# Scaled R of group 0 read from SBUF, the float32 decay-column matmuls set beside the first layer, the last output row block in two column halves, and a new written-out order

## The chip, the cores and the metric

The kernel runs on one core of one Trainium2 chip. The metric is device microseconds of one execution. The core has five engines with instruction streams of their own: TensorE (PE, whose weight loads are listed apart as PEld), VectorE (DVE), ScalarE (ACT), GpSimd (POOL) and SyncE (SP), which here issues most of the DMA transfers. Tensors are worked on in SBUF; matmuls write to PSUM.

## The reference, cut to what matters

```python
# attention: batch 4, 8 heads, 768 steps, head size 48
for t in range(S):
    cur = einsum('bhd,bhe->bhde', u * k[t], v[t])
    y[t] = einsum('bhd,bhde->bhe', r[t], state + cur)
    state = w[:, :, None] * state + einsum('bhd,bhe->bhde', k[t], v[t])
# feed-forward on the 3072 rows of y (384 wide), 2048 hidden units
h = x @ w_in
g = where(h >= 1, h, where(h <= -1, 0, (h + 1)**2 / 4))
out = g @ w_out
```

The recurrence decays by `w` per step, for each head and channel. All inputs and the output are float32.

## The kernel before, in words

**Tiling.** The 768 steps are cut into 6 chunks of 128, and the 4 batches into 2 pairs. A *group* is one chunk of one batch pair: 12 groups, numbered 0 to 11, each with two *units* (one batch each), so that units 0 and 1 are group 0. Within a chunk the recurrence becomes matmuls: R is scaled by `w` to the power (t - 64) (table `Wup`), K by the power (63 - t) (table `Wdn`), and then the 128x128 product of scaled K and scaled R, masked to the lower triangle, times V gives the part inside the chunk; scaled R times the state gives the part from earlier chunks. The diagonal term with `u` is worked out apart and added.

**The steps of a group**, by the names of the order table: `LR`, `LK`, `LV` load R, K, V (line 252; half a group is 192 KB); `Rs`, `Ks` scale; `KU`, `RKU` multiply K by u and R by that; `us` sums it over each head (293); `V` casts V to bf16; `B` multiplies V by that sum (302); `TR`, `TK` or `T` transpose on PE (319), `cR`, `cK`, `c` copy the result to SBUF; from group 4 on `RT`, `KT` transpose by DMA instead (307); `A` is the product of K and R (359), `AT` masks it (373 for a half, 368 for a whole unit); `Sp` is K times V (394), `Tm`, `Tmg` and `decayg` update the state, `sbf`, `sbfg` cast it; `Y` is the result in PSUM (421, 427), `y`, `yg` add the diagonal term; `X` and `xc` transpose it on PE (449), or `xcg` by DMA (456), giving `xT`. The feed-forward part follows per group and quarter q of the hidden units: `m` is the first layer (464; 12 matmuls of 256 columns into `hp`), `r`, `s`, `g` the activation (475 on ACT or 472 on DVE, 484 on ACT, 487 on DVE), `M` the second layer for one unit and one quarter (499; 4 matmuls of 384 columns), `o`/`og` the copy out of PSUM, `st`/`stg` the store (515, 518).

**PSUM.** `m`, `M` and, later in the program, all others use four pairs of banks, given as the number behind the slash. `m0.3/0` uses pair 0 again after `m0.0/0`, so it waits until `g0.0` has read `hp`. In the first two groups most other tiles use four single banks b0 to b3; `m1.0/3` and `m1.2/2` take the same space later, so they wait for the last reader of these.

**The set-up.** `ln` takes the logarithm of w (one row). `bw` (206) and `bu` (210) spread that and u over 128 partitions by float32 matmuls with one row of ones. ACT makes the tables: `WdnS` (224) and `WupS` (221) into SBUF, `Wdn` (218) and `Wup` (214) a second time into PSUM, from where the scaling of group 0 reads them. `wq` (232) makes the decay column, w to the power 128 as a column, by four float32 matmuls of one column; `wE` and `wC` spread it to the mask `wCm`, which `Tm` needs. `Z` are matmuls of zeros (526); `WI` and `WO` load the weights of the two layers through POOL's own DMA queue, in three and two pieces (243, 246). Piece 0 of `WI` serves quarter 0, piece 1 quarter 1, piece 2 quarters 2 and 3.

**What sets the order.** The string ORDER is the program: each word is one step, each engine executes its words in the order in which they stand there, and waits come only from data and from buffers (SLOTS gives the buffers of each kind). `=V`, `=A`, `=G` choose DVE, ACT or POOL. Loads, DMA transposes and stores all stand in SP's queue, in order.

Of the kernel before, what the change touches and what calls it, by code (L numbers as in the profile page):

```python
# [25 lines left out]
TK0/0 Wup/1 Rs0.0=V TR0/3 LK1.1 cK0=A WupS KU0.1=G KU0.0=V RKU0.0=G cR0=A KU1.0=G LV0.1 Rs0.1=V Z2 TR1/1 A0/03 LV1.0
LV1.1 WI0 WI1 WI2 us0.0 cR1=A TK1/1 cK1=A AT0.1 Z4 A1/13 Rs1.0=V LR2.0 LR2.1 Rs1.1=V V0.1 AT1.0 V0.0 Z9 TR3/1 B0.0=G
AT1.1 RKU0.1=V wE AT0.0 wC=A us0.1 Z7 Y1/3 TR2/0 B0.1=G Y0/2 y0 y1 cR2=A RKU1.0=G Z8 X0/2 Z4 TK2/3 X1/0 Ks1.1=G xc0=A
Sp1/2 cK2=A xc1=A Z7 TK3/3 cK3=A Tm1 A2/20 m0.0/0 cR3=V us1.0 AT2.1 AT2.0 r0.0=A A3/31 AT3.1 KU1.1=G RKU1.1=G m0.1/1
V1.0 s0.0=A B1.0=G Sp2/2 AT3.0 us1.1 r0.1=A Tm2 Y2/3 y2 g0.0 V1.1 X2/0 LK2.0 Y3/1 B1.1=G s0.1=A LK2.1 Sp0/2 Sp3/3  # L30
xc2=V LK3 y3 WO0 m0.3/0 r0.3=A s0.3=A g0.1 X3/1 Tm0 xc3=V m0.2/1 LR3 LV2.0 Tm3 m1.1/2 g0.3 r1.1=V m1.0/3 m1.2/0 Ks2=G
r0.2=A s0.2=A g0.2 sbf2=A s1.1=A r1.0=A s1.0=A sbf3=A g1.1 m1.3/1 r1.2=V WO1 KU2=G LV2.1 M0.00/2 M0.10 M0.11 M0.01
g1.0 M1.00/3 M1.10 M1.11 M1.01 Rs2=G s1.2=A g1.2 T5/0 RKU2=G LK4 r1.3=A s1.3=A g1.3 T4/1 LV3 Ks3=G M0.02 M0.03 LR4 us2
c5=V A5/0 KU3=G Rs3=G c4=V A4/1 AT5 sbf1=A M1.02 M0.12 M0.13 AT4 T6/0 sbf0=A V2 Y4/1 Y5 B2=G og0=A T7/2 c6=A RKU3=G
c7=A yg2 LV5 M1.12 Sp4/0 Sp5 M1.03 X5/2 Tmg2 decayg2=G X4/1 M1.13 A6/0 xc4=A xc5=V m2.0/2 A7/1 us3 AT6 m2.1/0 og1=A
LK5 LR5 V3 Y6/3 B3=G sbfg2=A r2.0=A AT7 Y7 m2.2/1 s2.0=A Ks4=G yg3 xcg3 m2.3/3 g2.0 Rs4=G r2.1=A s2.1=A g2.1 LV4
r2.2=A s2.2=A KT4 M2.00/2 M2.10 M2.01 M2.11 r2.3=A KU4=G RT4 RKU4=G g2.2 s2.3=A LK6 m3.0/0 us4 M2.02 m3.1/1 LR6 M2.12
LV6 r3.0 s3.0=A Ks5=G g2.3 M2.03 Sp6/3 Sp7 M2.13 g3.0 m3.2/0 Rs5=G Tmg3 r3.1 s3.1=A RT5 og2=A g3.1 V4 AA4/23 AT9 Ks6=G
r3.2 s3.2=A KT5 m3.3/1 M3.00/3 M3.10 V5 B4=G AT8 Y8/2 Y9 r3.3 g3.2 s3.3=A LK8 M3.11 M3.12 M3.01 M3.02 yg4 AA5/20 g3.3
M3.13 M3.03 xcg4 m4.0/1 LR7 KU5=G RKU5=G AT10 LK7 decayg3=G sbfg3=A Rs6=G og3=A us5 LV7 B5=G KU6=G RKU6=G r4.0 Sp8/2  # L40
Sp9 AT11 Tmg4 m4.1/3 s4.0=A Y10/0 Y11 yg5 m4.2/2 r4.1 g4.0 xcg5 RT6 s4.1=A g4.1 m4.3/0 r4.2 us6 KT6 r4.3 LV8 s4.2=A
g4.2 M4.00/1 M4.10 M4.01 stg0 M4.11 s4.3=A g4.3 m5.1/3 Ks7=G V7 M4.12 LR8 decayg4=G Rs7=G AA6/02 M4.02 M4.03 M4.13
r5.1 AT12 m5.0/0 s5.1=A V6 sbfg4=A stg2 AT13 Y12/2 Y13 stg1 og4=V m5.2/1 g5.1 KU8=G B6=G yg6 m5.3/3 KT7 xcg6 Sp10/2
r5.0 s5.0=A KU7=G RKU7=G r5.2 s5.2=A Sp11 g5.0 M5.00/0 M5.10 M5.11 M5.01 RT7 Tmg5 LR9 g5.2 M5.02 Ks8=G LK9 us7 r5.3
s5.3=A V8 g5.3 decayg5=G sbfg5=A LK11 m6.1/2 r6.1 s6.1=A stg3 Rs8=G RT8 B7=G AA7/13 M5.03 Rs9=G M5.12 M5.13 AT15
m6.0/3 og5=A r6.0 AT14 g6.1 Y14/0 Y15 yg7 RKU8=G KU9=G xcg7 s6.0=A m6.3/1 m6.2/2 g6.0 Sp12/0 Sp13 r6.3 r6.2 s6.2=A us8
KT8 M6.00/3 M6.10 M6.11 M6.01 Tmg6 LV11 B8=G s6.3=A m7.1/0 RT9 LK10 g6.2 M6.02 LV10 g6.3 AA8/21 M6.03 r7.1 M6.12 M6.13
decayg6=G AT16 sbfg6=A RKU9=G LR10 s7.1=A AT17 Ks9=G og6=A m7.0/2 Sp14/1 Sp15 Y16/3 Y17 r7.0 g7.1 m7.2/0 KU11=G s7.0=A
Tmg7 yg8 xcg8 Ks10=G KT9 r7.2 m7.3/1 g7.0 M7.00/3 s7.2=A g7.2 M7.10 M7.11 LV9 r7.3 M7.01 KU10=G s7.3=A g7.3 V10 stg6
decayg7=G M7.12 RKU10=G sbfg7=A M7.02 AA9/02 M7.13 m8.0/1 stg5 LR11 AT18 Rs10=G V9 KT10 M7.03 r8.0 s8.0=A AT19 RT10  # L50
og7=V us9 B9=G m8.1/0 m8.2/2 r8.1 s8.1=A Y18/3 Y19 stg7 g8.0 m8.3/1 yg9 r8.2 Rs11=G RKU11=G M8.00/3 M8.10 xcg9 g8.1
M8.11 s8.2=A g8.2 Sp16/0 Sp17 Tmg8 stg4 RT11 r8.3 s8.3=A M8.01 M8.02 g8.3 m9.0/2 r9.0 s9.0=A us10 decayg8=G AA10/01
AT21 Ks11=G M8.03 sbfg8=A B10=G AT20 M8.12 M8.13 g9.0 og8=A m9.1/1 Y20/0 Y21 r9.1 m9.2/3 s9.1=A yg10 xcg10 g9.1 r9.2
M9.00/0 m9.3/2 KT11 s9.2=A stg8 M9.10 M9.11 Sp18/1 Sp19 r9.3 g9.2 s9.3=A M9.01 Tmg9 M9.02 g9.3 m10.0/3 decayg9=G V11
# [512 lines left out]
```

## Time and profile before

| what | value |
|---|---|
| median of 3 runs | 174.38 us (174.08, 174.38, 174.93) |
| the profiled execution | 173.8 us, its span 172.0 us |
| DVE, ACT, POOL busy | 76%, 76%, 68% of the span |
| DMA, mean over the span | 164 GB/s |
| first layer, 576 matmuls | 69.1 us |
| second layer, 384 matmuls | 68.4 us |

The profiled execution took 1.8 us more than its span, which is the time outside the first and last instruction. Busy time on PE is an overlap of pipelined matmuls, so the start of one group of matmuls against the start of the next says more than its length. Rows of the timeline give the start, the length, the engine with the line, what is written and read, a count, and in brackets the idle time just ahead with what ended it.

### The profile page before, as it was taken

What the parts mean: (1) busy time and instruction counts of PE and PEld (TensorE: products, weight loads), DVE (VectorE), ACT (ScalarE), POOL (GpSimd) and SP (SyncE); (2) the same over time, 40 slices, a digit from 0 to 9 for tenths busy, and PEclk for the clock granted to TensorE, in tenths of its full rate; (3) what the DMA queues carried; (4) which work ended last, traced back from release to release, by engine and by line L of the source; (5) the groups of instructions that cost most, each with busy time, mean ns of one, the idle gap of its engine ahead of it and who ended that gap; (6) DMA issues with size and microseconds to landing.
All of it is one profiled execution on the core that took longest, in us unless ns stands there. A gap on an engine that the chain in (4) does not pass through costs nothing.

```text
span 172.0 us, 4014 instructions
## 1 busy us (share of the span) xinstructions
PE 163.7 (95%) x1658; PEld 130.9 (76%) x1658; DVE 130.6 (76%) x149; ACT 130.0 (76%) x150; POOL 117.1 (68%) x85
## 2 busy tenths in 40 slices
PE   7989968999999999989999999999999999999991
PEld 5768768956889778588787797696897787888850
DVE  4578798988687688859799779885889958873751
ACT  4356588991699899289979878689695896988941
POOL 3496755998589959999999998999577804300000
PEclk9999999999999999999999999999999999999999
DMA  5999999999995999999999998998999034130022
GB/s 106 198 187 191 199 203 197 221 195 203 174 190 88 213 188 175 188 204 150 200 312 197 185 215 174 219 173 168 308 195 219 4 60 138 43 98 0 8 91 91
DMA packets 103591, 28.26 MB, mean 164 GB/s; under 512 B 98834, under 2 KB 102676, under 8 KB 103572
## 3 DMA queue, kind: packets, MB, share of 16 engines
q1 hardware_dynamic: 101824, 24.85, 79.6%
q0 software_dynamic: 1744, 3.15, 10.0%
...
q10 hardware_dynamic: 4, 0.00, 0.0%
...
## 4 chain that ended last, share of the span: by engine, by line
PE 81%; DMA 5%; SPq 4%; ACT 3%; POOL 2%; DVE 2%; issue 1%; DVEq 0%; POOLq 0%
PE hp L464 36%; PE op L499 34%; SPq L252 4%; PE A L359 3%; DMA Vi<-in_v_dram 3%; DMA xT<-y 2%; PE Y L427 2%; PE Y L421 2%; PE Sp L394 2%; ACT pt L475 1%; ACT Vb L111 1%; POOL V L302 1%; PE T L319 1%; DVE g L487 1%; POOL RKU L271 1%
## 5 line engine op out<-in xcount | busy, mean ns | idle before, releaser
L464 PE MATMUL hp<-xT,w_in 128*128 128x256 bf16 x576 | 69.1, 273 | 0.9 <-DMA xT<-y 0.5
L499 PE MATMUL op<-w_out,g 128*128 128x384 bf16 x384 | 68.4, 326 | 0.0
L487 DVE SCALAR_TENSOR_TENSOR g<-sq,hp 128x1024 bf16<-128x1024 bf16 x48 | 57.9, 1215 | 13.2 <-ACT sq L484 13.2
L464 PEld LDWEIGHTS <-w_in 128*128 128x128 bf16 x576 | 61.9, 114 | 4.2 <-issue 1.2
L475 ACT ACTIVATE pt<-hp 128x1024 f32<-128x1024 f32 x46 | 46.9, 1020 | 14.0 <-PE hp L464 14.0
L499 PEld LDWEIGHTS <-g 128*128 128x128 bf16 x384 | 36.3, 98 | 21.3
L484 ACT ACTIVATE sq<-pt 128x1024 bf16<-128x1024 f32 x46 | 48.3, 1057 | 1.2
L368 DVE TENSOR_TENSOR AT<-A,umask 128x1024 bf16<-128x1024 f32 x20 | 23.7, 1219 | 5.2 <-PE A L359 5.2
L271 POOL TENSOR_TENSOR Ks<-Ki,Wdn 128x768 bf16<-128x768 f32 (+1 forms) x12 | 20.2, 1684 | 7.4 <-DMA Ki<-in_k_dram 3.7
L302 POOL TENSOR_TENSOR V<-Vb,diag 128x768 f32<-128x768 bf16 (+1 forms) x14 | 18.1, 1292 | 10.2 <-DVE diag L293 4.4
L271 POOL TENSOR_TENSOR RKU<-Ri,KU 128x768 f32<-128x768 f32 (+1 forms) x13 | 21.2, 1631 | 1.2 <-DVE KU L271 0.8
L405 POOL TENSOR_TENSOR state<-Tm,wCm 128x768 f32<-128x768 f32 x8 | 14.6, 1822 | 10.6 <-DVE Tm L402 10.6
L271 POOL TENSOR_TENSOR KU<-Ki,u_sb 128x768 f32<-128x768 f32 (+1 forms) x13 | 21.2, 1632 | 0.4 <-DMA Ki<-in_k_dram 0.3
L271 POOL TENSOR_TENSOR Rs<-Ri,Wup 128x768 bf16<-128x768 f32 x10 | 18.2, 1824 | 0.0
L439 DVE TENSOR_TENSOR y<-Y,V 128x768 bf16<-128x768 f32 x10 | 9.6, 956 | 5.9 <-PE Y L427 3.3
L111 ACT CAST Vb<-Vi 128x768 bf16<-128x768 f32 (+1 forms) x14 | 10.2, 734 | 4.8 <-DMA Vi<-in_v_dram 4.8
L293 DVE TENSOR_REDUCE diag<-RKU 128x16 f32<-128x768 f32 (+1 forms) x14 | 11.6, 830 | 1.5 <-POOL RKU L271 1.5
L111 ACT COPY o<-op 128x768 f32<-128x768 f32 (+1 forms) x9 | 6.9, 764 | 6.4 <-PE op L499 6.3
L111 ACT CAST state_bf<-state 128x768 bf16<-128x768 f32 (+1 forms) x12 | 8.5, 717 | 3.7 <-POOL state L405 3.7
L427 PE MATMUL Y<-Vb,AT 128*128 128x48 bf16 x192 | 10.2, 185 | 0.4 <-ACT Vb L111 0.4
L427 PEld LDWEIGHTS <-AT 128*128 128x128 bf16 x192 | 9.3, 97 | 0.7 <-issue 0.5
L402 DVE TENSOR_TENSOR Tm<-Sp,state 128x768 f32<-128x768 f32 x8 | 7.6, 956 | 2.7 <-PE Sp L394 2.7
...
## 6 DMA issues: line engine op xcount, KB each, us to landing
out_dram<-o SPq DMA_DIRECT2D x11, 384.0 KB, 3.9
Ki<-in_k_dram SPq DMA_DIRECT2D x9, 384.0 KB, 6.0
Ri<-in_r_dram SPq DMA_DIRECT2D x9, 384.0 KB, 6.1
Vi<-in_v_dram SPq DMA_DIRECT2D x9, 384.0 KB, 5.0
w_out<-in_moe_w_out_dram POOLq DMA_DIRECT2D x2, 768.0 KB, 8.6
Ki<-in_k_dram SPq DMA_DIRECT2D x6, 192.0 KB, 3.9
Ri<-in_r_dram SPq DMA_DIRECT2D x6, 192.0 KB, 4.6
Vi<-in_v_dram SPq DMA_DIRECT2D x6, 192.0 KB, 5.4
```

What stands on the lines that cost most here:

```text
L111: nc.scalar.copy(out, in_) if e == "A" else engines[e].tensor_copy(out, in_)
L271: engines[e].tensor_mul(part(out)[:, :, :, :D], part(a), rep(b, j1 - j0) if len(b.shape) == 3 and b.shape[1] == H else part(b))
L293: nc.vector.tensor_reduce(d[:, hs], tiles["RKU", g][:, hs, :], AX.X, ALU.add)
L302: engines[e].tensor_mul(t[:, hs, :], tiles["V", g][:, hs, :], tiles["diag", g][:, hs].unsqueeze(2).to_broadcast([P, n, D]))
L368: nc.vector.tensor_mul(t.rearrange("p i n t -> p (i n) t"), tiles["A", n].rearrange("p i (n t) -> p (i n) t", t=P), umask.unsqueeze(1).to_ ...
L405: engines[e].tensor_mul(states[g % BP], tiles["Tm", g], flat(wCm).unsqueeze(1).to_broadcast([P, UNITS, DM]))
L427: nc.tensor.matmul(Y[:, h * D : (h + 1) * D], AT[:, i, p, :], V[:, j * H + h, :], start=(c == 0), stop=True, skip_group_check=True,)
L464: nc.tensor.matmul(hp[:, f, :], w_in_sb[wi][:, i, wo * FG * P + f : (wo + 1) * FG * P : FG], tiles["xT", g][:, :, i, :], start=(i == 0), s ...
L475: nc.scalar.activation(t, tiles["hp", g, q], AF.Relu, bias=0.5, scale=0.5)
L484: nc.scalar.activation(t, p, AF.Square)
L487: nc.vector.scalar_tensor_tensor(out=make("g", ("g", g, q), [P, FG, TOK], BF16), in0=tiles["sq", g, q], scalar=1.0, in1=tiles["hp", g, q], ...
L499: nc.tensor.matmul(tiles[key][:, k, :DO], tiles["g", g, q][:, f, j * P : (j + 1) * P], w_out_sb[wi][:, wo, f * DO : (f + 1) * DO], start=( ...
```

## The change

1. `Wup` (the PSUM copy) goes out of the order; `WupS` stands ahead, and both units' scaled R of group 0 are read from the SBUF table, as those of all other groups are. `Wdn` in PSUM stays.
2. `wq` moves from behind `bu` to the place between the last transpose of group 0 (`X1`) and `m0.0`; `wE` and `wC` follow there.
3. In group 11 each unit's output is kept in two column halves in the two banks of its pair: 192-column matmuls, 8 in place of 4 for each quarter. The last step is cut into `MA`, `MB` with a copy and a store for each half (`oA`, `oB`, `stA`, `stB`).
4. The order is written anew throughout: other PSUM pairs, other places of loads and of zeros (60 of them before, 64 now), and some steps on another engine, among them `KU0.1`, `KU2`, `KU3` and `Ks3` from POOL to DVE, `uS` from DVE to ACT, `Rs1.1` from DVE to POOL. The number of loads, stores of whole groups, and all arithmetic stay.
5. The buffer `idle` shrinks from 512 to 128 columns. The new steps `HR`, `HK`, `Zq` are defined but not in the order.

```diff
-Zs/0 ln Z19 bw/1 LK0.0 bu/0 uS=V LK1.0 LR0.0 LK0.1 LR0.1 LV0.0 wq/2 WdnS Ks1.0=G LR1.0 LR1.1 Wdn/3 Ks0.0=V Ks0.1=V
+Zs/1 LV0.0 LR0.0 LR1.0 ln LK0.0 Z9 bw/0 LK0.1 bu/2 WupS LR0.1 Rs0.0=V Rs1.0=V Z2 TR0/1 uS=A Wdn/2 LV0.1 KU0.0=V
...
-M11.10/0
-M11.11 g11.2 stg10 r11.3 s11.3=A M11.00/3 M11.01 M11.12 M11.02 g11.3 M11.13 M11.03 o11.1=V st11.1 o11.0=A st11.0
+M11.00/0 M11.01 s11.3=A og10=V g11.3 M11.10/3 stg10 M11.11 M11.02 M11.03 M11.12 o11.0=V MA11.13 st11.0 MB11.13
+oA11.1=A oB11.1=V stA11.1 stB11.1
...
-    idle = const.tile([P, 512], BF16, name="idle")
+    idle = const.tile([P, P], BF16, name="idle")
...
-    def do_M(e, b, g, jq):
+    def do_M(e, b, g, jq, halves=(0, 1)):
...
-        key, k = (("op", g, j), 0) if last else (("op", g), j)
+        key = ("op", g, j) if last else ("op", g)
...
+        for i, o0, o1 in [(i, i * DO // 2, (i + 1) * DO // 2) for i in halves] if last else [(j, 0, DO)]:
+            for f in range(FG):
+                nc.tensor.matmul(
+                    tiles[key][:, i, : o1 - o0], tiles["g", g, q][:, f, j * P : (j + 1) * P], w_out_sb[wi][:, wo, f * DO + o0 : f * DO + o1],
+                    start=(q == 0 and f == 0), stop=(q == nQ - 1 and f == FG - 1),
+                )
...
+    def half_out(e, g, j, i):
+        cols = slice(i * DO // 2, (i + 1) * DO // 2)
+        copy(e, make("o", ("o", g, j), [P, UNITS, DO], F32)[:, 0, cols], tiles["op", g, j][:, i, : DO // 2])
...
+    def half_st(g, j, i):
+        cols = slice(i * DO // 2, (i + 1) * DO // 2)
+        nc.sync.dma_start(out=rows_out(g, j, j + 1)[:, :, cols], in_=tiles["o", g, j][:, 0:1, cols])
```

PE, the place of the decay column `wp`. Before, it stands in the set-up, between the two spreading matmuls and the first transposes (`TK`):

```order
L526 MATMUL z<-idle 128x128
L206 MATMUL lwp<-lnw,ones 128x384
L210 MATMUL up<-u_row,ones 128x384
L232 MATMUL wp<-ones,lnw 128x1 x4
L319 LDWEIGHTS Ks
L319 MATMUL TK<-ident,Ks 128x128
```

PE now, where the first layer (`hp`) begins; `X` are the transposes of group 0's result, one set for each unit:

```order
L566 MATMUL z<-idle 128x128
L460 LDWEIGHTS y
L460 MATMUL X<-ident,y 128x128
...
L405 MATMUL Sp<-Vb,Ks 128x96
...
L460 MATMUL X<-ident,y 128x128
L233 MATMUL wp<-ones,lnw 128x1 x4
L475 LDWEIGHTS w_in_116
L475 MATMUL hp<-xT,w_in_116 128x256
```

The four float32 matmuls have moved from ahead of all transposes to the spot just ahead of the first layer's first matmul.

POOL, from its first product to the loads of the first layer's weights (`w_in_116`, `w_in_117`, `w_in_118` are the pieces 0, 1 and 2), before:

```order
L271 TENSOR_TENSOR Ks<-Ki,Wdn 128x8x48
L271 TENSOR_TENSOR KU<-Ki,u_sb 128x384
L271 TENSOR_TENSOR RKU<-Ri,KU 128x384
L271 TENSOR_TENSOR KU<-Ki,u_sb 128x384
L243 DMA w_in_116<-in_moe_w_in_dram 128x3x512
L243 DMA w_in_117<-in_moe_w_in_dram 128x3x512
L243 DMA w_in_118<-in_moe_w_in_dram 128x3x1024
L302 TENSOR_TENSOR V_277<-Vb,diag 128x384 x2
```

and now:

```order
L282 TENSOR_TENSOR RKU<-Ri,KU 128x384
L244 DMA w_in_116<-in_moe_w_in_dram 128x3x512
L244 DMA w_in_117<-in_moe_w_in_dram 128x3x512
L282 TENSOR_TENSOR Ks<-Ki,Wdn 128x8x48
L282 TENSOR_TENSOR KU<-Ki,u_sb 128x384
L313 TENSOR_TENSOR V_287<-Vb,diag 128x384 x2
L244 DMA w_in_118<-in_moe_w_in_dram 128x3x1024
L282 TENSOR_TENSOR Ks<-Ki,Wdn 128x8x48
```

One product stands ahead of pieces 0 and 1 in place of four, while piece 2 has moved behind both products `B` of group 0 (`V` here).

DVE, up to the first two results `g` of the activation, before:

```order
L293 TENSOR_REDUCE diag<-RKU 128x8
L398 TENSOR_TENSOR state<-Sp,wCm 128x384
L435 TENSOR_TENSOR y<-Y,V_436 128x384
L487 SCALAR_TENSOR_TENSOR g<-sq,hp 128x1024
L111 COPY xT<-X 128x384
L435 TENSOR_TENSOR y<-Y,V_436 128x384
L487 SCALAR_TENSOR_TENSOR g<-sq,hp 128x1024
```

and now, from the masks of unit 2 on (`A_433`, `A_434` are the two halves of unit 3, and the two `y` of group 1 follow behind):

```order
L384 TENSOR_TENSOR AT<-A_382,umask 128x512
L409 TENSOR_TENSOR state<-Sp,wCm 128x384
L304 TENSOR_REDUCE diag<-RKU 128x8 x2
L112 COPY TT<-TK 128x512
L498 SCALAR_TENSOR_TENSOR g<-sq,hp 128x1024
L384 TENSOR_TENSOR AT<-A_434,umask 128x512
L384 TENSOR_TENSOR AT<-A_433,umask 128x512
L498 SCALAR_TENSOR_TENSOR g<-sq,hp 128x1024
L446 TENSOR_TENSOR y<-Y,V_457 128x384
```

Unit 3's copy now stands ahead of the first `g` and its two masks between the two `g`, where before one copy and one `y` of group 1 stood between them; both `y` come after.

More of the change, by code (lines that the diff above doesn't have):

```diff
@@ L24 @@
 ORDER = """
-Zs/0 ln Z19 bw/1 LK0.0 bu/0 uS=V LK1.0 LR0.0 LK0.1 LR0.1 LV0.0 wq/2 WdnS Ks1.0=G LR1.0 LR1.1 Wdn/3 Ks0.0=V Ks0.1=V
[L26 to L54, printed above, removed]
@@ new lines @@
+RKU0.0=G cR0=A LK1.0 Ks0.0=V WdnS LK1.1 Ks0.1=V Z16 TK0/0 WI0 KU0.1=V cK0=A Rs0.1=V V0.0 Z8 TK1/0 WI1 LR1.1 us0.0
+TR1/1 RKU0.1=V A0/23 cR1=A AT0.1 LV1.0 LV1.1 Ks1.0=G AT0.0 V0.1 cK1=V KU1.0=G us0.1 Z18 A1/01 TK2/3 AT1.0 B0.0=G cK2=A
+AT1.1 Z6 Y0/0 TR2/2 B0.1=G y0 Y1/3 cR2=A WI2 Sp0/1 y1 Z5 X0/2 Sp1/0 xc0=A X1/3 xc1=V Ks1.1=G wq/2 wE m0.0/0 RKU1.0=G
+LR2.0 wC=A Tm1 KU1.1=G A2/23 r0.0=A m0.1/1 AT2.0 Rs1.1=G AT2.1 s0.0=A Tm0 TK3/1 RKU1.1=G us1.0 TR3/0 sbf1=A r0.1=A
+cR3=A us1.1 cK3=V A3/12 g0.0 s0.1=A LK2.0 LK2.1 AT3.1 AT3.0 V1.0 g0.1 B1.0=G m0.3/0 V1.1 WO0 Sp2/3 LR2.1 Y2/0 Y3/2
```

59 lines of the change are left out of this document (50 added, 9 removed).

## Prediction

> **What bounds the kernel now.** I read the page first, then PE's timeline, then what the other engines wait for in the opening, then the end. All starts and lengths are in us from the span's start.
>
> ```profile
> PE 163.7 (95%) x1658; PEld 130.9 (76%) x1658; DVE 130.6 (76%) x149; ACT 130.0 (76%) x150; POOL 117.1 (68%) x85
> PEclk9999999999999999999999999999999999999999
> ```
>
> PE is busy for 95% of the span, so only the stretches where it stands or turns over zeros can give time back. PE's timeline shows where they are:
>
> ```profile
> 4.85 1.48 PE L210 MATMUL up<-u_row,ones 1*128 1x384 f32 x2
> 6.13 1.70 PE L232 MATMUL wp<-ones,lnw 1*128 1x1 f32 x8
> 7.76 0.61 PE L319 MATMUL TK<-ident,Ks 128*128 128x128 bf16 x4
> ...
> 12.58 1.14 PE L526 MATMUL z<-idle 128*128 128x128 bf16 x9
> 13.52 0.63 PE L319 MATMUL TR<-ident,Rs 128*128 128x128 bf16 x4
> ...
> 14.69 0.53 PE L427 MATMUL Y<-Vb,AT 128*128 128x48 bf16 x8
> ...
> 15.31 0.36 PE L427 MATMUL Y<-Vb,AT 128*128 128x48 bf16 x8
> 15.52 0.61 PE L526 MATMUL z<-idle 128*128 128x128 bf16 x8
> ...
> 19.04 1.50 PE L464 MATMUL hp<-xT,w_in 128*128 128x256 bf16 x12
> ...
> 25.00 1.47 PE L464 MATMUL hp<-xT,w_in 128*128 128x256 bf16 x12
> ...
> 27.09 6.73 PE L464 MATMUL hp<-xT,w_in 128*128 128x256 bf16 x60 [0.45 <-DVE g L487]
> 33.65 5.36 PE L499 MATMUL op<-w_out,g 128*128 128x384 bf16 x32
> ...
> 73.56 1.47 PE L464 MATMUL hp<-xT,w_in 128*128 128x256 bf16 x12 [0.47 <-DMA xT<-y]
> ```
>
> The first layer begins at 19.04, the second at 33.65. From 27.09 to the end PE stands once, for 0.47 ahead of `m4.0`. Opening, that wait and the tail are all there is to win.
>
> The timeline also shows a slow start that the clock row does not: nine zeros start 0.104 apart at 12.58 (next start 13.52), while eight take 0.61 in all at 15.52; eight Y matmuls take 0.53 at 14.69 and 0.36 at 15.31. Between these PE doubles its pace, at about 14.9. "Cold" and "warm" below mean this.
>
> **The opening, part by part.** The costs of single steps and the transfers:
>
> ```profile
> 5.09 0.58 ACT L224 ACTIVATE Wdn<-lwp,dn_col 128x384 f32<-128x384 f32 x1 [1.73 <-PE lwp L206]
> 10.75 2.47 POOL L243 DMA_DIRECT2D w_in<-in_moe_w_in_dram  x3
> 8.61 4.67 DMA Vi<-in_v_dram
> L475 ACT ACTIVATE pt<-hp 128x1024 f32<-128x1024 f32 x46 | 46.9, 1020 | 14.0 <-PE hp L464 14.0
> L484 ACT ACTIVATE sq<-pt 128x1024 bf16<-128x1024 f32 x46 | 48.3, 1057 | 1.2
> L487 DVE SCALAR_TENSOR_TENSOR g<-sq,hp 128x1024 bf16<-128x1024 bf16 x48 | 57.9, 1215 | 13.2 <-ACT sq L484 13.2
> L373 DVE TENSOR_TENSOR AT<-A,umask 128x512 bf16<-128x512 f32 x8 | 5.2, 686 | 1.1 <-PE A L359 1.1
> L435 DVE TENSOR_TENSOR y<-Y,V 128x384 bf16<-128x384 f32 x4 | 2.2, 557 | 0.7 <-POOL V L302 0.3 <-PE Y L427 0.3
> L111 ACT COPY TT<-TR 128x512 bf16<-128x512 bf16 x3 | 1.8, 586 | 0.6 <-PE TR L319 0.6
> L271 POOL TENSOR_TENSOR RKU<-Ri,KU 128x384 f32<-128x384 f32 x3 | 3.0, 1002 | 0.9 <-DVE KU L271 0.8
> w_in<-in_moe_w_in_dram POOLq DMA_DIRECT2D x2, 384.0 KB, 6.9
> w_in<-in_moe_w_in_dram POOLq DMA_DIRECT2D x1, 768.0 KB, 11.9
> ```
>
> *Loads.* V0.1 was the tenth load and landed at 8.61 + 4.67 = 13.28; now it is the seventh, about three loads earlier, and no longer last. K0.0 falls from first to fourth, but U is ready only after `bu` (4.85 + 1.48 = 6.33) anyway. ACT copies it (about 0.6) to 6.95, DVE multiplies (0.56) to 7.5, POOL makes `RKU0.0` (1.0) to 8.6, and then issues pieces 0 and 1 of w_in: 2.1 earlier than 10.75. At 6.9 to landing they are there by about 15.5 and 17, ahead of their use. Piece 2 goes behind K1.0's two products and both `B` (four half steps of up to 1.0 after K1.0, the eighth load, at about 11.2), to about 15, 2.6 later than now; at 11.9 that is 26.9, but that figure holds the wait behind pieces 0 and 1 in the same queue, which now start 2.1 earlier; I take 23. It is needed at 23.9 (below).
>
> *Scaled R from SBUF.* `WupS` takes `WdnS`'s place at 5.09, so R is scaled by 6.25 instead of after 7.77. SBUF or PSUM as source makes no difference that I count: the row for scaled R of group 0 from PSUM is like those of `y` from PSUM (0.56). One table exponential (0.58 on ACT) goes. The gain is only that `TR0` starts at 6.4.
>
> *PE to the first layer.* From 6.4 PE's own queue is the bound: four transposes cold take 0.43 (0.61 less the overlap), a zero 0.105, eight A about as much as eight Y, 0.55. TR0, 16 zeros, TK0, 8 zeros, TK1, TR1, A0, 18 zeros, A1, TK2, 6 zeros: 5 x 0.43 + 48 x 0.105 + 2 x 0.55 = 8.3, so Y0 at about 14.7. Then warm, at about 0.2 each: Y0, TR2, Y1, Sp0, 5 zeros, X0, Sp1, X1 and two short waits for `y` bring X1 to 16.6. `wp` uses X0's bank and waits for ACT's copy, to 16.95.
>
> *The decay column.* Cold it takes 7.76 - 6.13 = 1.63. No row shows it warm. Every bf16 row halves at the step, so I take 0.85 (16.95 to 17.8), and 1.63 as the upper end. Without it the first layer would start when `xT` of unit 1 is copied, at 17.2: it costs 0.6 there, at most 1.4. What it leaves free in its old place is in the earlier `TR0`.
>
> The Trainium skill ("TensorE: Matmul & The Clock Gate", LDWEIGHTS) gives a weight load as columns / 1.2 ns whatever the pace: 107 ns for 128 columns, about half of one of the eight records here (1.63/8 = 0.204). By that rule the column would not shrink and the sum would be 0.8 higher.
>
> *First layer to second.* Start 17.8, against 19.04: a lead of 1.2. What frees `hp` decides how much of it survives:
> - `m0.0` ends 19.3; r 1.02, s 1.06: 21.4. ACT then casts a state (a half step, 0.5), `r0.1` to 22.85, copies `TR3` (0.59) to 23.4, `s0.1` to 24.4, V1.0 and V1.1 to 25.2.
> - DVE: masks of unit 2 from 19.6 (2 x 0.65), `Tm0`, two `us` and `cK3` (half steps like `y`, 0.48 apart) to 22.7, `g0.0` (1.21) to 23.85. So `m0.3` at 23.9 (25.00 before). `A3` waits for the `TR3` copy, to 23.75; its masks to 25.15, `g0.1` to 26.3.
> - `m0.2` at 26.3 (27.09 before). `y2`, `Tm2`, `y3`, `Tm3` behind `g0.1` on DVE (4 x 0.48) put X3 at 27.8 and its copy at 28.5. `m1.0` needs that space: 28.55. The old kernel would start the same step at 27.09 + 1.31 = 28.4, since it had X3 done before.
>
> So the lead is gone: four quarters of group 1 (4 x 1.31; 60 matmuls took 33.65 - 27.09) end at 33.8 and the second layer starts there, against 33.65: **+0.15**. w_out lands as before, its first piece being issued about 25.5:
>
> ```profile
> 25.26 0.76 POOL L246 DMA_DIRECT2D w_out<-in_moe_w_out_dram  x1
> w_out<-in_moe_w_out_dram POOLq DMA_DIRECT2D x1, 768.0 KB, 8.3
> ```
>
> 25.5 + 8.3 = 33.8: just in time. With the decay column at 1.63 all of this shifts by 0.8.
>
> **The middle.** POOL loses KU2, KU3 and Ks3 to DVE, which has the room at 76%:
>
> ```profile
> L271 POOL TENSOR_TENSOR KU<-Ki,u_sb 128x768 f32<-128x768 f32 x10 | 18.2, 1823 | 0.0
> ```
>
> Three such steps, 5.5 of POOL time, come out ahead of group 4's products, so `B4`, `yg4` and the DMA transpose for `m4.0` move up; the 0.47 wait should go. DVE's own steps, about 1 each by twice the half step, lie between activations whose next matmuls use other pairs. I count **-0.4** (0 to -0.47). New waits of that size are possible, since every step has moved; I count none.
>
> **The tail.**
>
> ```profile
> 163.31 5.21 PE op L499 x32
> 168.54 0.48 ACT o L111
> ...
> 169.05 0.34 SPq L515 DMA_DIRECT2D out_dram<-o  x1
> ...
> 169.40:169.80 0.40, 0.00 (x0) 0.00 (x0) 0.00 (x0) 0.00 (x0) 0.00 (x0) 1.00 1.02 357
> 169.80:170.20 0.40, 0.00 (x0) 0.00 (x0) 0.00 (x0) 0.00 (x0) 0.00 (x0) 1.00 0.93 327
> 170.20:170.60 0.40, 0.00 (x0) 0.00 (x0) 0.00 (x0) 0.00 (x0) 0.00 (x0) 1.00 0.66 234
> ```
>
> 32 matmuls of 384 columns take 5.21, or 0.163 each; 12 of 256 take 1.31, or 0.109: time goes by columns, so two of 192 cost what one of 384 did, and I count 0 (up to 0.3 for 32 extra instructions). The last copy halves, 0.48 to about 0.35: -0.13. The two last stores of 192 KB move through the engines one after the other from 169.4 to 170.6 (1.2 in all); now only 96 KB leave after the last copy, the rest ahead: -0.3 (0 to -0.45). Together **-0.45**.
>
> **Sum.** +0.15 - 0.4 - 0.45 = -0.7. The profiled execution took 173.8, giving 173.1; the median of the runs shown, 174.38, lies 0.58 above that execution, so on its footing the forecast is 174.38 - 0.7 = **173.7**. About 0.5% (0.87) is what a measurement of this kernel can tell from no change: 173.5 to 175.25 counts as the same. The bounds of the terms (+0.8 for the column, 0.4 for the wait, 0.3 each for halves and store) give this case's own range of 173.2 to 174.6.
>
> **Rivals.**
>
> *The decay column costs its cold price.* For: no row shows float32 warm. Against: all else halves. 173.7 + 0.8 = 174.5, the same.
>
> *The lead of 1.2 survives.* The chain above is tight at three places: the `TR3` copy behind `r0.1`, `g0.0` behind `cK3`, `y3` behind `g0.1`. If ACT and DVE run them with less waiting, the second layer starts up to 1.2 + 0.15 earlier; about two thirds gives 172.8, faster. Against: each step's length is from rows.
>
> *PE stays cold longer (slower).* The step at 14.9 came after PE had been almost unbroken from 12.0 with zeros, A and Y. Now zeros stand in other blocks with transposes between. The Trainium skill (same page, the HAM clock gate, and PE-mode transpose) has a free-running activity window of about 3.4 us and says that transposes do not count as activity; by that, the moment may differ from run to run. Cold PE work runs at half pace, so each 1 of delay costs about 0.5, less some 0.4 hidden in waits. To lose 0.5% needs 0.87 + 0.7 = 1.55 over the forecast, or a step later than about 18.8; at 22 it would cost (22 - 14.9)/2 - 0.4 = 3.1: 176.8.
>
> *w_in starves the loads.* Pieces 0 and 1 run 2.1 earlier, so V1.0 and V1.1 (again 11th and 12th) now share the engines with them:
>
> ```profile
> 10.85 0.99 SPq L252 DMA_DIRECT2D Vi<-in_v_dram  x1
> 11.88 0.99 SPq L252 DMA_DIRECT2D Ri<-in_r_dram  x1
> ...
> Ri<-in_r_dram SPq DMA_DIRECT2D x1, 192.0 KB, 12.8
> ```
>
> The load behind them took 12.8 under w_in. Then V1.1 lands at 10.85 + 12.8 = 23.65, 1.0 ahead of its cast at about 24.65: hidden. Three later still, 2.0 would show: 175.7, slower.
>
> **Chances.** Forecast 0.45 (0.15 faster, 0.30 the same), column at cold price 0.2 (0.17 the same, 0.03 slower), lead survives 0.2 (faster), cold PE 0.08 and starved loads 0.07 (slower). Together faster 0.35, same 0.47, slower 0.18. A range of 172.6 to 175.2 takes in the first three cases and leaves the two slower ones out.
>
> **What would show it.** In the changed kernel's PE timeline: `wp` near 17 with 0.85 to the next start; first `hp` at 17.8; `hp` again at 23.9 and 26.3; the next at 28.5; `op` first at 33.8; no idle ahead of `m4.0`; the last copy about 0.35 and the span's end about 3.0 - 0.45 after PE's end. Wrong if `op` starts before 33 or after 34.8, or if new waits of over 0.5 stand on PE after 35.

## The result and the profile after

| what | before | after |
|---|---|---|
| median, 4 runs each | 174.36 us (174.08 to 174.93) | **176.73 us** (176.49 to 176.93) |
| ratio, 95% interval | | 1.0125 [1.0097, 1.0152] |
| the profiled execution, its span | 173.8, 172.0 | 176.49, 174.7 |
| granted clock, mean | 1.000 | 0.988 |
| second layer starts | 33.65 | 34.94 |
| from there to PE's end | 134.85 | 136.25 |
| from PE's end to the span's end | 3.52 | 3.53 |

Slower, and above the range of 172.6 to 175.2. The last three rows say where the 2.7 us went by which the profiled spans differ (the medians differ by 2.4): 1.29 in the opening, 1.39 in the middle, 0.01 in the tail. Medians here and below are of all runs of a kernel, while a ratio leaves out runs more than 1.5% above the fastest of the same kernel.

The page of after. PE is still busy for 94%, but the clock row, all nines before, now has a dip at its sixth and seventh slice (each 4.4 long, so about 22 to 31):

```profile
PE 163.8 (94%) x1694; PEld 132.3 (76%) x1694; DVE 133.7 (76%) x153; ACT 130.1 (74%) x149; POOL 111.8 (64%) x82
...
PEclk9999978999999999999999999999999999999999
```

PE's timeline of the opening, with the start, the length, the work, the count and in brackets the idle time ahead and its releaser:

```profile
9.89 0.56 PE L330 MATMUL TK<-ident,Ks 128*128 128x128 bf16 x4
10.29 0.39 PE L330 MATMUL TR<-ident,Rs 128*128 128x128 bf16 x4
...
16.05 1.05 PE L233 MATMUL wp<-ones,lnw 1*128 1x1 f32 x8
17.03 1.17 PE L475 MATMUL hp<-xT,w_in 128*128 128x256 bf16 x9
...
22.54 0.40 PE L370 MATMUL A<-TT 48*128 48x128 bf16 x8 [1.23 <-ACT TT L112]
23.75 2.64 PE L475 MATMUL hp<-xT,w_in 128*128 128x256 bf16 x12 [0.81 <-DMA w_in<-in_moe_w_in_dram]
26.18 0.53 PE L405 MATMUL Sp<-Vb,Ks 128*128 128x96 bf16 x4
...
29.67 5.43 PE L475 MATMUL hp<-xT,w_in 128*128 128x256 bf16 x48 [0.45 <-DVE xT L112]
34.94 2.28 PE L512 MATMUL op<-w_out,g 128*128 128x384 bf16 x13
```

The start is better than forecast: four transposes go from 0.56 to 0.39 at 10.3 (14.9 before), and the first layer starts at 17.03 (19.04 before). All of that lead is lost by 29.67. `m0.3` waits 0.81 for w_in and then takes 2.43 to the next start (23.75 to 26.18), where twelve such matmuls take 1.31 at full pace. Two windows of that stretch show the clock beside it (PE's busy time is the first column after the length; the granted clock is the third number from the end):

```profile
20.51:23.92 3.41, 1.18 (x18) 0.92 (x18) 3.41 (x7) 3.41 (x7) 0.00 (x0) 1.00 1.22 215
23.92:27.33 3.41, 3.41 (x35) 2.74 (x34) 1.67 (x3) 1.24 (x2) 3.37 (x5) 0.50 0.88 159
```

PE worked 1.18 of 3.41, and then the clock stood at 0.50 for as long. The piece of w_in that `m0.3` needs was issued at 14.72 and took 9.0, so it landed at 23.7:

```profile
14.72 0.80 POOL L244 DMA_DIRECT2D w_in<-in_moe_w_in_dram  x1
w_in<-in_moe_w_in_dram POOLq DMA_DIRECT2D x1, 768.0 KB, 9.0
```

In the middle the wait of 0.47 ahead of `m4.0` is gone, and two others have come, on the DMA transposes of R and K of groups 7 and 8:

```profile
98.42 0.62 PE L370 MATMUL A<-RT,KT 48*128 48x128 bf16 x16 [0.52 <-DMA RT<-Rs]
111.53 0.62 PE L370 MATMUL A<-RT,KT 48*128 48x128 bf16 x16 [0.75 <-DMA KT<-Ks]
```

That is 1.27 of waits in place of 0.47. POOL, 5.3 less busy, was no earlier for it: it stood waiting for a load of R (3.64 ahead of 37.16), and then for ACT's cast of V, which came at 43.68 behind ACT's own work. The V of group 2 began at 44.60 (41.94 in before).

```profile
44.60 1.47 POOL L313 TENSOR_TENSOR V<-Vb,diag 128x768 f32<-128x768 bf16 x1 [5.61 <-ACT Vb L112]
```

The tail of after. PE ends at 171.18; the first half's copy (ACT) starts only then, and the second's (DVE) behind it:

```profile
165.09 6.09 PE L512 MATMUL op<-w_out,g 128*128 128x384 bf16 x68
171.22 0.32 ACT L112 COPY o<-op 128x192 f32<-128x192 f32 x1 [3.68 <-PE op L512]
171.56 0.82 SPq L539 DMA_DIRECT2D out_dram<-o  x2
171.57 0.36 DVE L112 COPY o<-op 128x192 f32<-128x192 f32 x1 [1.11 <-ACT o L112]
```

### The profile page after: what moved, and what is told of

It reads as the page before. It is cut to its first block, busy times and chain, and to the rows that moved or that the text cites. A ratio compares the mean times of both kernels' runs of the same rounds, so it can differ in the third digit from the quotient of the medians.

```text
span 174.7 us, 4088 instructions
## 1 busy us (share of the span) xinstructions
PE 163.8 (94%) x1694; PEld 132.3 (76%) x1694; DVE 133.7 (76%) x153; ACT 130.1 (74%) x149; POOL 111.8 (64%) x82
## 4 chain that ended last, share of the span: by engine, by line
PE 68%; POOL 12%; DMA 9%; issue 4%; SPq 3%; DVE 2%; ACT 0%; POOLq 0%
PE op L512 30%; PE hp L475 29%; DMA w_in<-in_moe_w_in_dram 5%; POOL KU L282 4%; SPq L253 3%; PE A L370 3%; DMA Ki<-in_k_dram 3%; POOL V L313 2%; PE Y L438 2%; POOL Rs L282 2%; POOL state L416 2%; DMA KT<-Ks 2%; PE Y L432 2%; PE Sp L405 1%; POOL Ks L282 1%
## 5 line engine op out<-in xcount | busy, mean ns | idle before, releaser
L475 PE MATMUL hp<-xT,w_in 128*128 128x256 bf16 x576 | 70.0, 276 | 1.3 <-DMA w_in<-in_moe_w_in_dram 0.8
L512 PE MATMUL op<-w_out,g 128*128 128x384 bf16 (+1 forms) x416 | 67.8, 314 | 0.0
L512 PEld LDWEIGHTS <-g 128*128 128x128 bf16 x416 | 38.5, 98 | 20.0
L282 POOL TENSOR_TENSOR Rs<-Ri,Wup 128x768 bf16<-128x768 f32 (+1 forms) x11 | 19.3, 1750 | 7.5 <-DMA Ri<-in_r_dram 7.4
L282 POOL TENSOR_TENSOR Ks<-Ki,Wdn 128x768 bf16<-128x768 f32 (+1 forms) x11 | 18.5, 1679 | 2.8 <-PE Sp L405 1.8
L282 POOL TENSOR_TENSOR KU<-Ki,u_sb 128x768 f32<-128x768 f32 (+1 forms) x10 | 16.6, 1664 | 0.3 <-DMA Ki<-in_k_dram 0.3
L112 ACT COPY o<-op 128x768 f32<-128x768 f32 (+1 forms) x8 | 5.9, 743 | 6.8 <-PE op L512 6.8
```

The lines of the kernel that those rows point to most:

```text
L112: nc.scalar.copy(out, in_) if e == "A" else engines[e].tensor_copy(out, in_)
L282: engines[e].tensor_mul(part(out)[:, :, :, :D], part(a), rep(b, j1 - j0) if len(b.shape) == 3 and b.shape[1] == H else part(b))
L475: nc.tensor.matmul(hp[:, f, :], w_in_sb[wi][:, i, wo * FG * P + f : (wo + 1) * FG * P : FG], tiles["xT", g][:, :, i, :], start=(i == 0), s ...
L512: nc.tensor.matmul(tiles[key][:, i, : o1 - o0], tiles["g", g, q][:, f, j * P : (j + 1) * P], w_out_sb[wi][:, wo, f * DO + o0 : f * DO + o1 ...
```

## The experiments

The theory after the result: the opening loses to the late piece of w_in and the low clock, the middle to DMA transposes that come late, and the tail gains nothing since the halves share a tile. The rivals are named in each expectation. All ratios are to the kernel before, run on the same chip.

### The opening

**e1: the third piece of w_in early.** After, with

```diff
-TK1/0 WI1 LR1.1
+TK1/0 WI1 WI2 LR1.1
```

> The changed kernel with one DMA issue moved: piece 2 of w_in is issued on POOL directly behind piece 1 instead of behind both products B of group 0. Theory (piece 2, landing at 23.7, holds m0.3 back and PE's wait before it drops the granted clock to 0.5): piece 2 lands at about 21.5 to 22, m0.3 starts at about 23.1 right behind g0.0, the clock stays at 1.0 or drops for less long, the second layer starts at about 33.4 to 34.0 instead of 34.94, total 1 to 1.5 us less than the changed kernel. Rival (the waits for the copy of TR3 and for g0.0 alone drop the clock): m0.3 earlier by 0.7, but still cold, total less by at most 0.7. Rival (the loads of V1 are starved by the earlier piece 2): the V1 casts wait past 25, and nothing is won.

176.09 us, ratio 1.0077 [1.0042, 1.0112].

```profile
23.52 1.47 PE L475 MATMUL hp<-xT,w_in 128*128 128x256 bf16 x12
...
33.08 1.47 PE L475 MATMUL hp<-xT,w_in 128*128 128x256 bf16 x12 [0.77 <-DVE g L498]
34.39 1.79 PE L512 MATMUL op<-w_out,g 128*128 128x384 bf16 x10
```

The wait on w_in and the low clock are gone from this profile, and the second layer starts 0.55 earlier. A new wait of 0.77 on `g` took up the rest. An early piece does not secure the clock: two of e1's six runs had a mean of 0.986 and 0.989. Later kernels with this opening tell the two apart. In h3, h5, h6, h7, h9 and h10 there is no wait on w_in either, and yet the clock fell to 0.50 for 3.41; in e1, h1 and h2 it did not. The second layer starts at 34.04 to 34.50 in the first group (35.05 in h3, where other steps moved too) and at 34.06 to 34.41 in the second. In h6, with the clock fallen, it reads:

```profile
28.77 5.43 PE L475 MATMUL hp<-xT,w_in 128*128 128x256 bf16 x48 [0.45 <-DVE xT L112]
34.04 2.28 PE L512 MATMUL op<-w_out,g 128*128 128x384 bf16 x13
```

The first layer's start also moves between these kernels (16.86 to 17.47). Counted from there, the second layer comes 17.91 later in after, 17.2 to 17.6 in the first group (17.6 in h3) and 16.9 in the second. So the late piece and the low clock are two causes: with the piece early and the clock low, 0.3 to 0.7 of the microsecond between after and e1 is back; with the clock up and the piece late (e2, below, 16.9), all of it. Their prices overlap, they are read from one profile of each kernel, and the waits on `g` and, later, on w_out hide a part.

The wait on `g` is that of a longer product. `KU2` on DVE took 2.72 in e1, beside POOL's `Rs` of the same group, and ended 0.83 behind it; in after it began when `Rs` had ended (28.83 and 1.82), and took 0.95. In e1 two rows, and then after's:

```profile
29.18 2.72 DVE L282 TENSOR_TENSOR KU<-Ki,u_sb 128x768 f32<-128x768 f32 x1
29.25 1.82 POOL L282 TENSOR_TENSOR Rs<-Ri,Wup 128x768 bf16<-128x768 f32 x1
...
30.66 0.95 DVE L282 TENSOR_TENSOR KU<-Ki,u_sb 128x768 f32<-128x768 f32 x1
```

So e1 laid bare a wait that after does not have.

**e2: 40 zeros in the thin stretch.** After, with 6 zeros ahead of `TK3`, 22 ahead of `A3`, 12 ahead of `m0.3`.

> The changed kernel with 40 more matmuls of zeros where PE stood: 6 ahead of TK3, 22 ahead of A3, 12 ahead of m0.3 (into bank 3, free there). No data step moves. Theory (the low clock from about 23.7 to 26.6 comes from PE standing, and costs some 1.2 us): granted clock 1.0 throughout, m0.3 still at about 23.8 (it waits for piece 2) but 1.3 long instead of 2.4, second layer at about 33.7 instead of 34.94, total about 1.2 us less. Rival (the clock is not what costs, the second layer is held by data): second layer and total within 0.3 us of the changed kernel.

177.78 us, ratio 1.0188 [1.0135, 1.024]. The clock stayed up (0.997 to 1.000 in all four runs) and `m0.3` ran at full pace, at 24.01; the second layer started at 34.43, as in e1. So it was the thin PE work of this stretch that let the clock fall. The total rose all the same: waits on transposes came to 0.91 at 74.28 and 1.63 at 112.00, 1.27 more than the two of after. The lost microsecond is in the middle.

**e4: the decay column early.** After, with the column in place of 18 zeros:

```diff
-us0.1 Z18 A1/01
+us0.1 wq/3 wE wC=A A1/01
```

> The changed kernel with the decay column's four float32 matmuls, and the two ACT steps behind them, moved to just ahead of A1, in place of the 18 zeros there (PE stood 0.6 us there). Theory (piece 2 of w_in sets m0.3, so the column's place does not matter): the first layer starts at about 16.4 instead of 17.03, m0.3 stays at about 23.7, the stall ahead of it gets longer and the clock drops as before; total within 0.5 us of the changed kernel. Rival (the column at the first layer is what makes the change slow): total 0.7 to 1.0 us less.

176.29 us, ratio 1.0108 [1.0057, 1.016]. A miss: the first layer started at 17.82, later than in after, and the second at 35.74. The step to full pace still came early (at 11.3: `A` took 0.61 at 10.85 and 0.40 at 13.22; in this opening it came between 8.9 and 11.9 in the kernels that keep the zeros), and the column took 0.98. But then the clock fell to 0.50, from 14.75 to 18.16, and once more from 24.99 to 28.40:

```profile
13.22 0.40 PE L370 MATMUL A<-TT 48*128 48x128 bf16 x8
...
14.75:18.16 3.41, 2.87 (x34) 2.48 (x32) 2.05 (x5) 1.22 (x3) 3.39 (x5) 0.50 1.25 220
```

So here the 18 zeros, or the column in their place, decide whether the full pace lasts; that it comes early is not shown to hang on them. The profiled run was the slowest of the four (177.15), and two others had a mean clock as low, near 0.98. The column's price is read from after itself: 16.05 to 17.03.

**h2: the K*u product of group 2 behind the activation.** e1, with

```diff
-KU2=V s0.2=A m1.2/2 LK3 Ks2=G g0.2 r1.0=A
+s0.2=A m1.2/2 LK3 Ks2=G g0.2 KU2=V r1.0=A
```

> e1 (176.09 us) with the K*u product of group 2 on VectorE moved behind the last activation of its turn (g of unit 0, quarter 2). Theory: the 0.77 us wait of PE ahead of the fourth first-layer matmuls of unit 1 (33.08, on g) comes from that 0.95 us product, which stands ahead of that activation on VectorE; it goes, the second layer starts at about 33.65 as in the kernel before, and the time is about 175.4 us. Rival: the activation is late because ScalarE's square before it is late; then the wait keeps over 0.5 us and the time stays at 176.1.

176.57 us, ratio 1.0068 [1.0037, 1.0098]. The wait on `g` went, as the theory has it, and what was late next showed at once:

```profile
34.06 4.07 PE L512 MATMUL op<-w_out,g 128*128 128x384 bf16 x24 [0.80 <-DMA w_out<-in_moe_w_out_dram]
```

The first piece of w_out now ends last. `KU2`, behind `Rs` again, took 0.95. The second layer starts 0.33 earlier than in e1, but so did the first (17.11 against 17.47): from layer to layer it takes 16.95 and 16.92, so nothing of the 0.77 is left.

### The middle

**g1, g2: grafts.** g1 has the order of before up to `M0.00` and after's from there; g2 has after's up to `m2.0` and before's from there, with a whole tail.

> The order before up to the second layer's first step, then the changed kernel's order for all that is left (its tail too). Theory (the opening costs about 1.3 us at the second layer's start, of which about 0.5 are the low clock, and the rest of the order costs about another 1): second layer at about 33.7; new waits ahead of the A products of groups 7 and 8 as in the changed kernel; total 0.8 to 1.3 us over the kernel before. Rival (all is the opening's late start and what it pushes along): total within 0.4 us of the kernel before.

> The changed kernel's order up to the first layer of group 2, then the order before for all that is left, with its whole-row tail. Theory (as above): second layer at about 34.8, low clock once in the opening, then no waits over 0.6 us; total 1.0 to 1.6 us over the kernel before. Rival (the later order alone is slow): total within 0.5 us of the kernel before, since loads and POOL catch up.

g1 took 178.89 us, ratio 1.0189 [1.0156, 1.0223]; g2 180.87, ratio 1.0311 [1.0271, 1.035]. Both stall at the seam (1.98 on `g` at 35.78 in g1; 1.02 and 2.18 at 50.67 and 53.35 in g2) and lose clock there, so the totals settle nothing. One thing can be read from g1: its waits on RT (0.72 at 101.30) and KT (0.60 at 114.25) stand there behind the old opening too. They belong to the later part of the order.

**h1: the second piece of w_out later.** e1, with

```diff
-y3 WO1 Tm3
...
-LK3 Ks2=G g0.2
+y3 Tm3
...
+LK3 Ks2=G WO1 g0.2
```

> The kernel after with the third piece of w_in asked for early (e1) and, beside that, the second piece of w_out asked for behind Ks of group 2 in place of ahead of it. Base: e1, 176.09 us, with POOL idle 8.5 us ahead of V of group 2 (44.05), PE waits of 0.53 on RT (97.81) and 0.66 on KT (110.85). Theory 'weights starve the loads': with about 2 us between the two pieces of w_out the loads of groups 2 and 3 come 2 us earlier, POOL reaches the V of group 2 at about 42, as before, and both waits on the transposed tiles go: 174.9 us. Rival 'order': POOL reaches the K of group 7 behind a state update that waits for VectorE, and SyncE has loads and a y transpose queued ahead of the transposes of R and K; moving one load 50 us earlier leaves both waits as they are: 176.1 us, and up to 0.5 more if w_out then comes late for the second layer of group 0.

177.37 us, ratio 1.0131 [1.0085, 1.0176]. The waits on RT and KT stand as in e1 (0.47 at 97.93 and 0.54 at 110.96, in e1 0.53 and 0.66). But POOL did not become earlier either: the piece was issued only 1.8 later than in e1, and the V of group 2 came at 44.07 (44.05 in e1). So the run did not make the case that the theory speaks of, and the weights' part stays open here.

**h5: three steps moved.** e1, with `Ks7=G` moved ahead of `V6`, `RT8` ahead of `yg7`, and `KT7` ahead of `LR10`.

> e1 (176.09 us) with three moves in the middle: Ks of group 7 on POOL ahead of the state update of group 6 (into POOL's idle 2.24 us at 81.1), its transpose ahead of the load of R of group 10 on SyncE's queue, and the transpose of Rs of group 8 ahead of the transpose of y of group 7. Theory 'order': the waits of PE on RT (0.53 at 97.81) and on KT (0.66 at 110.85) are due to these places in the order; both go, and the time falls by about 1.2 us to 174.9, unless what is late next takes some of it back (half of it: 175.5). Rival 'weights starve the loads': the whole chain of loads is late since 30 us; the waits only move to another transpose, and the time stays within 0.3 us of 176.1.

176.34 us, ratio 1.0097 [1.0061, 1.0132].

```profile
109.86 1.50 PE L475 MATMUL hp<-xT,w_in 128*128 128x256 bf16 x12 [1.05 <-DMA xT<-y]
```

The wait on RT stayed (0.53 at 97.86). That on KT went, but the transpose of `y`, now behind that of R, was late instead, by more. SyncE's queue was the next suspect. In after it reads, at this place:

```profile
96.96 0.49 SPq L253 DMA_DIRECT2D Ki<-in_k_dram  x1
97.49 2.08 SPq L253 DMA_DIRECT2D Ri<-in_r_dram  x1
99.62 4.96 SPq L253 DMA_DIRECT2D Ki<-in_k_dram  x2
104.69 2.40 SPq L467 DMA_TRANSPOSE xT<-y  x1
107.20 1.24 SPq L318 DMA_TRANSPOSE RT<-Rs  x1
108.53 1.26 SPq L318 DMA_TRANSPOSE KT<-Ks  x1
```

Four loads of 384 KB in a row stand ahead of three transposes that PE needs. In before three loads stood there, and a store ahead of the transposes:

```profile
93.45 0.58 SPq L252 DMA_DIRECT2D Ri<-in_r_dram  x1
94.09 3.67 SPq L252 DMA_DIRECT2D Ki<-in_k_dram  x2
97.87 1.99 SPq L518 DMA_DIRECT2D out_dram<-o  x1
100.38 2.17 SPq L307 DMA_TRANSPOSE RT<-Rs  x1
102.66 1.22 SPq L456 DMA_TRANSPOSE xT<-y  x1
103.93 1.30 SPq L307 DMA_TRANSPOSE KT<-Ks  x1
```

**h8: the fourth load put into before.** Before, with `LK10` taken from behind `RT9` to directly behind `LK11`, ahead of the transposes of group 8, as after has it.

> The kernel before, with one load moved: K of group 10 directly behind that of K of group 11, so that it stands ahead of the transposes of group 8 on SyncE's queue, as in the kernel after. Theory 'queue': the transposes of R and of y and K there land some 1.5 to 2 us later, and PE, which in before waits nowhere between 90 and 112, waits 0.3 to 1.2 us there: 174.6 to 175.6 us beside 174.4 of the kernel before. Rival 'lateness': no wait comes, and the time is that of before.

175.18 us, ratio 1.0039 [1.002, 1.0059]. Where before does not wait, a wait has come:

```profile
94.91 5.59 SPq L252 DMA_DIRECT2D Ki<-in_k_dram  x3
101.01 2.99 SPq L518 DMA_DIRECT2D out_dram<-o  x1
104.11 1.31 SPq L307 DMA_TRANSPOSE RT<-Rs  x1
105.52 1.23 SPq L456 DMA_TRANSPOSE xT<-y  x1
...
108.55 1.50 PE L464 MATMUL hp<-xT,w_in 128*128 128x256 bf16 x12 [0.73 <-DMA xT<-y]
```

Against before on the same chip it costs 0.64 (175.18 - 174.54), and the interval of the ratio leaves out 1. That is near the one wait of 0.73, but the match is loose: the profiled run, the longest of its seven, also waited 0.84 ahead of `m4.0` (0.47 in before; it moves from run to run) and 0.25 on w_out at 34.07.

**h9: the same load taken out of after.** e1, with `LK10` behind `RT9`: the inverse of h8. **h10** is h9 with a whole tail.

> e1 (176.09 us) with one load moved, the inverse of h8: K of group 10 behind the transposes of groups 8 and 9 (where the kernel before has it) in place of ahead of them. Theory 'queue': three loads in place of four stand ahead of the transposes at 96 to 104 us, the transposes of y, R and K land up to 2 us earlier, and the wait of 0.54 to 0.66 on KT at 110.9 goes; the wait of 0.53 on RT at 97.8, which lies earlier, stays; 175.5 us. Rival 'given back later': as in h6, the load that stands later makes another transpose late between 112 and 126 us (a wait of 0.5 or more there), and the time is 176.1 or more.

> h9 with the tail of the kernel before, one copy and one store per unit: 0 to 0.1 us under h9, so 175.4 us by the theory and 176.0 by the rival. Both still hold the opening's 0.7 us and the wait on RT, so neither beats the kernel before (174.4).

h9 took 175.9 us, ratio 1.0091 [1.0061, 1.0122]; h10 176.1, ratio 1.0106 [1.0074, 1.0139]. PE's waits from 90 on in h9 are 0.41 on RT at 97.86, and:

```profile
121.81 0.62 PE L370 MATMUL A<-RT,KT 48*128 48x128 bf16 x16 [0.82 <-DMA KT<-Ks]
```

The wait at 111 is gone, by one load moved, and a wait on the K of another group stands ten microseconds later (1.09 at 121.99 in h10). It is not the moved load that comes due there: that transpose was issued at 117.00, behind three other loads, and at 116.89 in e1. There it was just in time for a PE that came at 121.72; in h9 PE came some 0.7 earlier and had to wait for it. The next tight place took the gain. The theory is borne out for the place; the rival, that the total stays, has the time, though the intervals of e1 and h9 would let half a microsecond hide. What putting this transpose ahead of its three loads would bring was not run.

**h6, h7: several loads later.** e1 with the transposes of group 7 ahead of `LR10`, `LK11` behind `RT9` and `LK10` behind `LR11`, both still ahead of `KT9` (`Ks7` ahead of `V6` too); h7 is h6 with a whole tail.

> e1 (176.09 us) with SyncE's queue put in another order between 82 and 110 us: Ks of group 7 on POOL ahead of the state update of group 6 and, on SyncE, the transposes of K and R of group 7 ahead of the load of R of group 10; the loads of K of groups 11 and 10 behind the transposes of group 8 in place of ahead of them. Theory 'queue': the new order puts three (82.1 to 89) and four loads (96.3 to 104.4) of 384 KB in a row ahead of transposes which PE needs next, on a queue that drains one such load in about 2 us; with two or three fewer ahead of them both waits (0.53 on RT at 97.8, 0.54 to 0.66 on KT at 110.9) go, and no wait of over 0.3 us stands on PE between 90 and 112: 174.9 us. Rival 'lateness': the transposes wait for POOL's and PE's work whatever stands ahead; then the waits stay or move to a transpose of y, as in h5, and the time stays within 0.3 us of 176.1.

> h6 and the tail of the kernel before, with one copy and one store per unit. If the tail in halves brings nothing, as e3 and f3 have it, 0 to 0.1 us under h6 (whole matmuls are 0.08 shorter); under both theories then 174.8 or 176.0 us. Under 174.2 would make it the fastest kernel of this study.

180.28 us, ratio 1.0312 [1.0267, 1.0358], and 180.79, ratio 1.0294 [1.0238, 1.0349]. Both old waits went, that on RT too, and far more came (h6; 0.86 on the transpose of `y` at 96.44 beside it):

```profile
124.36 0.62 PE L370 MATMUL A<-RT,KT 48*128 48x128 bf16 x16 [3.35 <-DMA KT<-Ks]
```

Here the moved loads do come due: both stand ahead of the K transpose of group 9, which was issued at 119.20.

**h3: all moves of e1, h1, h2 and h5 with a whole tail.**

> All of these moves together, and the tail of the kernel before (one copy and one store per unit) in place of halves: what is left of the change is the scaled R from the table, the column's place and the new order with its four misplaced points mended. If opening (0.77 us) and middle (1.2 us) add up as the theories have them, 176.1 - 0.8 - 1.2 = 174.1 us, no different from the kernel before (174.4) within its interval. If the waits only move, 175.5 us or more. Faster than 173.5 would mean that the change holds a gain that the misplaced points hid.

176.38 us, ratio 1.0056 [1.0024, 1.0089]. The gains did not add: `op` started at 35.05, the clock had fallen once more (0.990), and waits of 0.18 to 0.75 stood at four transposes between 74 and 111. No kernel of the study beat the one before by more than the noise (the least ratios are 0.9992).

### The tail and the scaled R

**e3: the whole tail in after** (one copy and one store per unit).

> The changed kernel with the old tail: 384-column matmuls for group 11, one copy and one store for each unit. Theory (the two half copies run one after the other behind all matmuls, so the split gives nothing): from PE's end to the span's end 3.4 to 3.6 us as in both kernels, total within 0.3 us of the changed kernel. Rival (the split saves 0.3 us of store time that is hidden in noise): the stretch behind PE's end grows to 3.8 us.

176.01 us, ratio 1.0106 [1.0062, 1.0149]. PE's end to the span's end: 3.48, against 3.53 with halves.

**f3: halves that wait for nothing in before.** Unit 0's last output in two PSUM pairs and two output buffers, with a copy and a store each.

> The kernel before, with only the tail changed: the last unit's row block in two halves in two PSUM pairs of their own, and two output buffers of their own, so that the first half's copy need not wait for the second half's matmuls. Theory (the changed kernel's split gave nothing because both halves share a pair and an output buffer and so their copies run one behind the other after all matmuls): here the first half's copy starts about 0.3 us before PE's end, and the stretch behind PE's end is 3.0 to 3.4 us instead of 3.5; total 0.1 to 0.4 us less than the kernel before. Rival (stores, not copies, set the end): the stretch stays at 3.4 to 3.6 us and the total is the same.

175.08 us, ratio 0.9992 [0.9968, 1.0017].

```profile
168.96 0.82 PE L517 MATMUL op<-w_out,g 128*128 128x192 bf16 x8
169.16 1.02 DVE L112 COPY o<-op 128x384 f32<-128x384 f32 x2 [1.21 <-PE op L500]
169.49 0.32 ACT L112 COPY o<-op 128x192 f32<-128x192 f32 x1 [2.80 <-PE op L517]
169.75 0.34 SPq L554 DMA_DIRECT2D out_dram<-o  x1
170.19 0.88 SPq L539 DMA_DIRECT2D out_dram<-o  x2
```

Now the first half's copy starts at 169.49, ahead of PE's end at 169.78, and yet the span ends 3.6 behind PE (173.4). Halves gain nothing even where they don't wait for each other: by the rows, what sets the end lies behind the copies, in the three stores that leave one after the other and their landing; no run tested that by itself. The profiled run also waited 1.06 ahead of `m4.0` and 0.51 on w_out.

**f4: scaled R from the SBUF table, alone, in before.**

```diff
-TK0/0 Wup/1 Rs0.0=V
+TK0/0 WupS Rs0.0=V
...
-cK0=A WupS KU0.1=G
+cK0=A KU0.1=G
```

> The kernel before, with the PSUM copy of the R table left out and the SBUF table made in its place, read by both scaled R of group 0. Theory (no path to the first layer runs through it: V0.1's landing does): first layer within 0.2 us of 19.04 and total the same within 0.3 us. Rival (source in SBUF or the exponential left out speeds the opening): total 0.3 to 0.6 us less.

175.01 us (before 175.34 on the same chip), ratio 0.9992 [0.9966, 1.0018], first layer at 19.17: no difference.

## Why the prediction was wrong

- **The start of the first layer** (forecast 17.8) was 0.8 too late. The step to full pace came at 10.3, not 14.7; how early is in part luck, as kernels with the same opening had it between 8.9 and 11.9. "No row shows it warm [...] so I take 0.85" was 0.98 for the column; its cold price of 1.63 was far off.
- **"I take 23. It is needed at 23.9"** is the first step that failed, in both halves. The piece landed at 23.7, and `A3` and `g0.0`, forecast for 23.75 and 23.85, were ready at 22.54 and 23.03. So a margin of 0.9 was a wait of 0.81, and PE stood, after a stretch already thin.
- **The pace after 23** was taken for granted. The rival on a cold PE had it at the start, where it didn't come; it came at 23.9 instead and cost 1.1 on `m0.3` alone (2.43 less 1.31). e1 took away both the wait and the low clock, e2 the low clock, h6 the wait alone; each brings back 0.5 to 0.9 of the 1.29 (`op` at 34.39, 34.43 and 34.04), and none all of it.
- **"DVE's own steps, about 1 each [...] lie between activations whose next matmuls use other pairs"** failed for `KU2` in e1 and e2, where it ran beside POOL's `Rs`: it took 2.72 and 2.63 and not 1, and h2 shows that the 0.77 on `g` in e1 is its. In after itself it took 0.95 and no wait on `g` stands there, so it is no part of after's loss. With +0.15 for the opening the forecast was short by 1.14.
- **"New waits of that size are possible [...] I count none"** is the second. The -0.4 for `m4.0` came (0.47), and 1.27 of new waits outweighed it, +0.80 in all; the middle took 1.39 more in place of 0.4 less. That `m4.0` did not wait is in part luck: in kernels with before's order the wait was 0.47 to 1.59, and in e2 and h2, with after's, it was back (0.91 and 0.32). The place of the new waits is SyncE's queue: h8 makes such a wait with one load, h9 and h6 take it away. The argument that less work on POOL brings its later work forward fell too: POOL waited for a load and for ACT, and its V of group 2 came 2.7 later than in before. Moving these loads back did not win time: in h9 PE met the next transpose that was just in time, in h6 one that the moved loads themselves held back. Why the wait on RT at 98 arises was only shown as a matter of the queue with several steps moved at once (h6), not of one load.
- **The tail, "-0.45"**, was 0. The copies of the halves wait for all matmuls and for each other in after; and f3 shows that even apart they bring nothing, so "now only 96 KB leave after the last copy, the rest ahead" isn't worth its -0.3.
- The remaining 0.6 of the middle (1.39 less 0.80) is PE time without a wait in the profile; of it 0.10 is the halves (64 x 0.083 against 32 x 0.163). The rest stays open, as does how much of the total is due to the clock: after's fourth run had a mean of 1.000 and took the longest, 176.93.
